# Digit counts for twelve columns at once, and two pairs of vector operations merged, in a fused attention, routing and MLP kernel

## The chip, the cores and the metric

One core of a Trainium2 chip runs the whole program. The metric is the device time of one execution in microseconds (us). The engines are named as in the profile: PE (TensorE; PEld is its weight loads), DVE (VectorE), ACT (ScalarE), POOL (GpSimd) and SP, whose queue issues the DMAs.

## The reference

Three stages follow each other, each on the output of the one before, all in float32:

```python
q_n, k_n = (rmsnorm(q, g_q), rmsnorm(k, g_k))        # 4 batches, 12 heads, 448 rows, 64 wide
attn = softmax(q_n @ k_n.T / 8)                      # per batch and head
x = (attn @ v)  laid out as 1792 rows of 768
order = np.argsort(-(x @ w_gate).flatten())          # 1792 tokens, 8 experts
for idx in order:                                    # a token takes its best expert that still
    tok, e = (int(idx) // E, int(idx) % E)           # has room; an expert holds cap = 224 tokens
    if assigned[tok] >= 0 or counts[e] >= cap:
        continue
    assigned[tok] = e
    counts[e] += 1
out[mask of e] = np.maximum(x[mask] @ w1[e], 0) @ w2[e]
h = out @ w_in;  result = (h * np.cos(h)) @ w_out    # 768 -> 2048 -> 768
```

The assignment must be exact: one swapped token changes whole rows of the result.

## The kernel before

**Attention** takes two heads (a pair) at a time, 24 pairs, 6 to a batch. Each pair has: squares and a root (`norm`, with a Newton iteration in `rsqrt`, lines 355 to 369) for the row norms of q and k; transposes (`turn`); a maximum per row (`shifts`: seven matmuls `s`, seven DVE reductions `cm`); scores, exponentials `pf` and their sums (`scores`, `weigh`); router logits of the pair, accumulated with the softmax sums in the one PSUM bank `dn`; reciprocals `r`, and the pair's output rows, transposed back into PSUM and scaled by `r` into `xk` (`tail`). A scaling of one pair is two DVE operations of 256 columns. Beside this work DVE, ACT and SP split the two MLP weights into high and low parts in pieces (`Narrow`, tiles `nr` and `na`, 38 pieces in this stage).

**Routing** needs for each expert its 224th best token. A token's logit is turned into an 18-bit and shorter digits; a histogram of the first digit comes from matmuls of two 0/1 matrices per column of 112 tokens (`ia == X` and `ib <= W`), 4 columns a batch. `Router.start` runs after the last pair of each batch: `best` (largest logit and its expert), `parts` (digits), `signs` (the two matrices of each column, half of the second ones as a sign on ACT; four matmuls into the bank `dn`) and an addition to `hist`. After batch 4, `quick` reads the histogram (`digits`: column totals `tot`, a matmul with `up`, a comparison `cmp`, a matmul with `ones`, a maximum `T`), and narrows to the next digit twice. The first routing stands between attention and the first expert with nothing beside it; the second one (expert 2) runs beside the first expert's matmuls, the others later.

**Order.** All steps are recorded, then a list planner (`Plan.run`) with its own costs writes each engine's instructions in the order it finds; the engines run their queues in that order. A change in any cost or count lets the planner place the whole attention stage anew. The second plan (experts and MLP) is laid out by itself.

Of the kernel before, what the change touches and what calls it, by code (L numbers as in the profile page):

```python
# [12 lines left out]
F32 = mybir.dt.float32  # L13
# [332 lines left out]
END = 20.0  # L346
NKQ = 5
NPA = 6
XKA = 0
XKL = 1  # L350
QND = False
SSA = 1


def rsqrt(v, out, x, t, g=None):
    v.tensor_scalar(out.bitcast(I32), x.bitcast(I32), 1, None, op0=ALU.logical_shift_right)
    v.tensor_scalar(out.bitcast(I32), out.bitcast(I32), -1, 0x5F3759DF, op0=ALU.mult, op1=ALU.add)
    for _ in range(3):
        if g is not None:
            g.tensor_tensor(t, out, out, op=ALU.mult)  # L360
            g.tensor_tensor(t, t, x, op=ALU.mult)
            g.tensor_scalar(t, t, -0.5, 1.5, op0=ALU.mult, op1=ALU.add)
            g.tensor_tensor(out, t, out, op=ALU.mult)
            continue
        v.tensor_tensor(t, out, out, op=ALU.mult)
        v.scalar_tensor_tensor(t, t, -0.5, x, op0=ALU.mult, op1=ALU.mult)
        v.scalar_tensor_tensor(out, t, 1.5, out, op0=ALU.add, op1=ALU.mult)


def attention(tc, P, R, ident, q, k, v, g_q, g_k, w_gate, x_dram, L, other):  # L370
# [4 lines left out]
    with ExitStack() as ctx:  # L375
# [30 lines left out]
        dns = ring("dn", 2, [128, CP])  # L406
        xks = ring("xk", 2, [CP, NC, 2 * UP * D])
        recs = ring("r", 3, [CP, NC, 2])
        abs_ = ring("ab", 1, [CP, 2, NC, 128], BF16)
        NPR = B * NP  # L410
        bt, b1, bs, bo, bd = bank("t", 2), bank("s1", 2), bank("st", 2), bank("po", 1), bank("dn", 1)

# [225 lines left out]
        def tail(P_, xk, e, r):  # L638
            xe, p = outs.pop(P_), bt()[0:CP]
            P.begin()  # L640
            for c in range(NC):
                pe.transpose(p[:, c * 128:(c + 1) * 128], xe[:, c * CP:(c + 1) * CP], ident)
            P.finish()
            for z in range(2):
                cs = slice(2 * z, 2 * z + 2)
                o = xk[:, cs, 2 * e * D:2 * (e + 1) * D].rearrange("p c (h d) -> p c h d", h=2)
                i = p.rearrange("p (c h d) -> p c h d", c=NC, h=2)[:, cs]
                if z < XKA or P_ >= NPR - XKL:
                    for c in range(2):
                        for h in range(2):  # L650
                            sc.activation(o[:, c, h], i[:, c, h], AF.Copy, scale=r[:, 2 * z + c, h:h + 1])
                else:
                    ve.tensor_tensor(o, i, r[:, cs].unsqueeze(3).to_broadcast([CP, 2, 2, D]), op=ALU.mult)

        roots_of, xk_of = {}, {}

# [20 lines left out]
        def finish(P_):  # L677
            if P_ < 0:
                return
            late = P_ >= NPR - LAST  # L680
            if P_ == NPR - 1:
                ve.tensor_reduce(part[:, :, :, H], part[:, :, :, 0:H - 2], AX.X, ALU.add)
            P.rush = END if P_ == NPR - 1 else 0.0
            r = rows(P_)
            if P_ % NP == NP - 1:
                b = P_ // NP
                ve.tensor_reduce(L[:, b * NC:(b + 1) * NC, :], part[:, :, :, (H - 2) * late:H + late], AX.X, ALU.add)
                R.start(abs_(), b)
            P.rush = 0.0
            pair(P_, r)  # L690

# [49 lines left out]

CP, NCOL, E, CAP = 112, 16, 8, 224
BIG = 1.5e38
SIGNS = 10
WIDE = 4096.0
SOON = 5.0
LATER = 10.0
# [3 lines left out]
class Router:  # L751
# [3 lines left out]
    def __init__(self, nc, pool, ident, L, rows):  # L755
# [32 lines left out]
        for s in range(8):  # L788
# [9 lines left out]
        iota(tmp[:, 144:272], [[-1, 128]], step=1)  # L798
        v.scalar_tensor_tensor(up.rearrange("p (e i) -> p e i", e=E), tmp[:, 144:272].rearrange("p (e i) -> p e i", e=E),
                               0.5, em.unsqueeze(2).to_broadcast([128, E, 16]), op0=ALU.is_ge, op1=ALU.mult)  # L800
        v.scalar_tensor_tensor(up, up.bitcast(F32), 2.0, self.ident, op0=ALU.mult, op1=ALU.add)


        row = t("row", [128, 1])
# [45 lines left out]
        v.tensor_copy(t("wd", [128, E]), w8)  # L850
        g.memset(t("rp", [128, 1]), float(CAP))
        g.memset(t("one", [128, 1]), 1.0)
        g.memset(t("rp2", [128, 1]), 2.0 * CAP)
        self.first_free()
        for name in ("m", "mx", "K", "F0", "F1", "Z", "X0", "X1", "X2", "W0", "W1", "W2", "G", "Q", "XF", "g"):
            t(name, [CP, NCOL])
        for name in ("X", "W"):
            t(name, [CP, NCOL, 2], BF16)
        for name in ("t0", "t1"):
            t(name, [CP, NCOL], I32)  # L860
# [1 line left out]
        t("hist", [128, 128])  # L862
        t("tot", [128, 2], F32R)
        t("acc", [128, 1])
        t("rpt", [128, 1])
        t("acc8", [128, E], BF16)
        t("cmp", [128, 128], BF16)
        for j in range(3):
# [66 lines left out]
    def parts(self, a, z, first=True, rest=True):  # L935

        P, v = self.P, self.nc.vector
        c = {n: P[n][:, a:z] for n in ("m", "mx", "K", "F0", "F1", "Z", "X0", "X1", "X2", "W0", "W1", "W2", "G", "t0", "t1")}
        k, K, i, j = c["m"].bitcast(I32), c["K"].bitcast(I32), c["t0"], c["t1"]
        if first:  # L940
            v.tensor_scalar(i, k, 31, -2147483648, op0=ALU.arith_shift_right, op1=ALU.bitwise_or)
            v.tensor_tensor(K, k, i, op=ALU.bitwise_xor)
        for q, (lo, n) in enumerate(((21, 7), (10, 7), (0, 6))):
            if not (rest if q else first):
                continue
            v.tensor_scalar(i, K, lo + n, 15, op0=ALU.logical_shift_right, op1=ALU.bitwise_and)
            v.scalar_tensor_tensor(c[f"X{q}"], c["mx"], -16.0, i, op0=ALU.mult, op1=ALU.add)
            v.tensor_scalar(j, K, lo, (1 << n) - 1, op0=ALU.logical_shift_right, op1=ALU.bitwise_and)
            v.tensor_scalar(c[f"W{q}"], j, 1.0 - (1 << n), None, op0=ALU.add)
        if not rest:  # L950
            return
        v.tensor_scalar(c["Z"], c["mx"], -16.0, 15.0, op0=ALU.mult, op1=ALU.add)
        for n, lo, z, add in (("F0", 21, 2047, 1.0), ("F1", 10, 0x3FFFFF, 2049.0), ("G", 0, 1023, 1.0)):
            v.tensor_scalar(i, K, lo, z, op0=ALU.logical_shift_right, op1=ALU.bitwise_and)
            v.tensor_scalar(c[n], i, add, WIDE, op0=ALU.add, op1=ALU.mult)
# [10 lines left out]
                                     row.rearrange("p (n k) -> p n k", k=2).unsqueeze(1).to_broadcast(sh),  # L966
                                     cols.unsqueeze(2).to_broadcast(sh), op=op)

    def signs(self, p, X, W, ab):

        nc, P = self.nc, self.P
        cols = X.shape[1]
        for c in range(cols):
            A, B, ib = ab[:, 0, c], ab[:, 1, c], P["ib"][0:CP]
            if c * SIGNS % 16 < SIGNS:
                nc.scalar.activation(B, ib, AF.Sign, bias=W[:, c:c + 1], scale=-1.0)
                nc.either("tensor_scalar", A, P["ia"][0:CP], X[:, c:c + 1], None, op0=ALU.is_equal)
            else:
                nc.either("tensor_scalar", B, ib, W[:, c:c + 1], 0.5, op0=ALU.is_le, op1=ALU.subtract)
                nc.either("tensor_scalar", A, P["ia"][0:CP], X[:, c:c + 1], 2.0, op0=ALU.is_equal, op1=ALU.mult)  # L980
            nc.tensor.matmul(p, A, B, start=(c == 0), stop=(c == cols - 1))

    def count(self, p, X, W, ab, n, whole=False):

        nc, P = self.nc, self.P
        for a in range(0, NCOL, 8):
            cs = slice(a, a + 8)
            self.match(ab[:, 0, cs], P["ia"][0:CP], X[:, cs], ALU.is_equal)
            self.match(ab[:, 1, cs, 0:n], P["ib"][0:CP, 128 - n:], W[:, cs], ALU.is_le)
            if whole:  # L990
                nc.begin()
            for c in range(a, a + 8):
                nc.tensor.matmul(p[:, 0:n], ab[:, 0, c], ab[:, 1, c, 0:n], start=(c == 0), stop=(c == NCOL - 1))
            if whole:
                nc.finish()

    def digits(self, p, n, T, signs=False):

        nc, P, v = self.nc, self.P, self.nc.vector
        rp = P["rp2" if signs else "rpt"]  # L1000
        if signs:
            v.tensor_copy(P["tot"], p[:, 0:1].to_broadcast([128, 2]))
        else:
            v.tensor_scalar(P["tot"], p[:, 0:1].to_broadcast([128, 2]), 0.5, None, op0=ALU.mult)
            v.tensor_tensor(rp, P["tot"][:, 0:1].bitcast(F32), P["rp"], op=ALU.add)
        pa = self.psum()
        nc.tensor.matmul(pa[:, 0:2], P["up"], P["tot"], start=True, stop=True)
        v.scalar_tensor_tensor(P["cmp"][:, 0:n], p[:, 0:n], pa[:, 0:1], rp.to_broadcast([128, n]), op0=ALU.add,
                               op1=ALU.is_ge, accum_out=P["acc"])
        v.tensor_scalar(P["acc8"], P["em"], P["acc"], WIDE, op0=ALU.mult, op1=ALU.mult)  # L1010
        pt = self.psum()
# [8 lines left out]
        v.tensor_tensor(P["X"], self.twice(P["XF"]), self.twice(P["Z"]), op=ALU.min)  # L1020
        v.scalar_tensor_tensor(P["W"], self.twice(F), T, self.twice(W), op0=ALU.is_equal, op1=ALU.mult)

    def start(self, ab, q):

        P, v, s = self.P, self.nc.vector, slice(4 * q, 4 * q + 4)
        self.best(self.L[:, s], s.start, s.stop, True)
        self.parts(s.start, s.stop, rest=q < 3)
        p = self.psum()
        self.signs(p[:, 0:128], P["X0"][:, s], P["W0"][:, s], ab)
        if q == 0:  # L1030
            v.tensor_copy(P["hist"], p[:, 0:128])
        else:
            v.tensor_tensor(P["hist"], P["hist"], p[:, 0:128], op=ALU.add)
# [1 line left out]
    def quick(self, first):  # L1035
# [4 lines left out]
        self.parts(12 * first, NCOL, not first)  # L1040
        if not first:
            p = ps()
            v.tensor_copy(P["X"], self.twice(P["X0"]))
            v.tensor_copy(P["W"], self.twice(P["W0"]))
            self.count(p, P["X"], P["W"], P["AB"], 128, True)
        self.digits(p, 128, T[0], first)
        self.narrow(P["F0"], T[0], P["X1"], P["W1"])
        p = ps()
        self.count(p, P["X"], P["W"], P["AB"], 128, not first)
# [514 lines left out]
```

## Time and profile before

| | us |
|---|---|
| median of 3 runs | 1137.42 (1134.14 to 1144.95) |
| profiled execution | 1139.09 |
| its span, first to last instruction | 1137.3 |
| attention, up to the last pair's logits | about 329 |
| first routing, up to the first gather of rows | about 329 to 357 |
| PE, DVE, ACT, POOL busy in the span | 1083.0, 873.6, 623.3, 248.6 |

Busy times are unions of spans. The matmuls' ends are modelled, so PE counts as busy while its pipeline only waits; the distance between equal matmuls of successive pairs is the better measure of pace. An idle time carries the engine whose result ended it.

### The profile page before, as it was taken

To read this page: it belongs to the slowest core of one execution; us is meant where nothing else is said; L and a number is where in the kernel's file an instruction comes from. 1 tells how busy PE (TensorE), PEld (TensorE's weight loads), DVE (VectorE), ACT (ScalarE), POOL (GpSimd) and SP (SyncE) were. 2 spreads that over 40 slices of the span, in tenths; PEclk is the share of its full clock that TensorE was granted. 3 is DMA by queue.
4 is the path that set the end of the run, shared out by engine and by line. 5 is a ranking of instruction groups with operands and counts; after the bars stand their busy time and mean duration, and the time that the engine had idled before them with its cause. 6 is when DMAs were issued, how large, how long until landed. Compare 5 with 4: busy or idle time off the path is not lost.

```text
span 1137.3 us, 20677 instructions
## 1 busy us (share of the span) xinstructions
PE 1083.0 (95%) x7272; PEld 880.7 (77%) x7272; DVE 873.6 (77%) x2250; ACT 623.3 (55%) x1512; POOL 248.6 (22%) x367
## 2 busy tenths in 40 slices
PE   7999999999966999999999999999999999999997
PEld 5555556555535898897988988899989798999887
DVE  7888989999988858999997885658889476856300
ACT  4787878865650337664566663337666236646300
POOL 3577777766511000000100000020000001000001
PEclk9899999999985899999999999999999999999999
DMA  6353455455653899789888669748866958666652
GB/s 146 106 156 113 147 185 163 163 163 180 210 215 94 237 217 304 254 230 371 282 222 199 226 211 283 243 155 219 230 207 221 323 195 235 193 217 210 240 185 93
DMA packets 172744, 234.34 MB, mean 206 GB/s; under 512 B 14112, under 2 KB 144608, under 8 KB 168032
## 3 DMA queue, kind: packets, MB, share of 16 engines
q1 hardware_dynamic: 170240, 222.01, 62.6%
q0 software_dynamic: 2400, 11.01, 3.0%
q8 instruction: 57, 0.93, 0.3%
q14 instruction: 47, 0.39, 0.1%
HBM read 196.37 MB, written 36.52 MB: 205 GB/s over the span
## 4 chain that ended last, share of the span: by engine, by line
PE 49%; DVE 10%; DMA 7%; issue 2%; SPq 1%; ACT 1%; POOL 0%; POOLq 0%; DVEq 0%; ACTq 0%
PE acc L47 47%; DMA ws<-in_moe_w_dram 3%; DVE wx L47 1%; PE rt L47 1%; DVE na L47 1%; DVE oh L47 1%; SPq L1301 1%; DMA ws<-in_moe_w_out_dram 1%; DMA xr<-x,idx 1%; PE tr L47 1%; DMA AB<-rows 1%; DMA wx<-w_out 1%; ACT wx L1310 1%; DVE AB L47 1%; DMA rows<-vm 1%
## 5 line engine op out<-in xcount | busy, mean ns | idle before, releaser
L47 PE MATMUL acc<-wx,gh 128*128 128x512 f32 (+1 forms) x896 | 226.8, 340 | 1.9 <-DMA wx<-w_out 1.9
L47 PE MATMUL acc<-x2h,wx 128*128 128x448 f32 x768 | 223.8, 369 | 0.0
L47 PEld LDWEIGHTS acc<-wx,gh 128*128 128x128 f32 x896 | 155.6, 190 | 22.6 <-issue 2.9
L47 PEld LDWEIGHTS acc<-x2h,wx 128*128 128x128 f32 x768 | 144.5, 188 | 11.5
L47 PE MATMUL acc<-wx,gl 128*128 128x512 f32 (+1 forms) x448 | 150.5, 336 | 0.0
L47 PE MATMUL acc<-x2l,wx 128*128 128x448 f32 x384 | 140.3, 365 | 0.0
L47 PE MATMUL acc<-gh,wx 128*128 128x448 f32 (+1 forms) x768 | 130.7, 326 | 4.0 <-DVE gh L47 2.9
L47 DVE TENSOR_TENSOR wx<-ws,wx 128x1024 fp32r<-128x1024 f32 (+1 forms) x96 | 104.6, 1089 | 33.8 <-ACT wx L1310 28.0
L47 POOL TENSOR_TENSOR pa<-pf,pf 112x448 f32<-112x448 f32 x94 | 111.7, 1208 | 71.9 <-ACT pf L47 71.7
L1261 POOL DMA_INDIRECT xr<-x,idx x16 | 17.4, 1085 | 502.6 <-DVE KX L47 133.9
L47 PEld LDWEIGHTS acc<-gh,wx 128*128 128x128 f32 x768 | 117.1, 192 | 12.9 <-DVE gh L47 3.2
L47 ACT ACTIVATE pf<-st 112x448 f32<-112x448 f32 x192 | 93.8, 539 | 42.0 <-PE st L47 40.4
L1310 ACT ACTIVATE wx<-ws 128x1024 fp32r<-128x1024 f32 (+1 forms) x96 | 91.0, 948 | 44.9 <-DMA ws<-in_moe_w_dram 23.1
L47 DVE TENSOR_REDUCE cm<-s 128x1 f32<-128x448 f32 x168 | 100.2, 619 | 18.7 <-PE s L47 16.6
L47 ACT ACTIVATE r<-r 128x448 f32<-128x448 f32 x128 | 74.0, 578 | 56.4 <-DVE r L47 54.5
L47 DVE SCALAR_TENSOR_TENSOR r<-r,acc 128x448 f32<-128x448 int32 (+1 forms) x128 | 77.7, 618 | 34.7 <-ACT r L47 33.5
L47 PE MATMUL acc<-xe,wx 128*128 128x448 f32 x576 | 91.9, 320 | 0.1
L47 PEld LDWEIGHTS acc<-wx,gl 128*128 128x128 f32 x448 | 85.0, 190 | 8.0
L47 PEld LDWEIGHTS acc<-xe,wx 128*128 128x128 f32 x576 | 86.2, 189 | 4.4 <-DVE wx L47 0.4
L47 PE MATMUL st<-qq,kk 64*112 64x448 f32 x576 | 88.7, 393 | 0.6 <-ACT pf L47 0.6
L47 ACT ACTIVATE oh<-oh 128x896 bf16<-128x896 bf16 x48 | 45.6, 950 | 75.9 <-DVE oh L47 75.8
L47 PE MATMUL po<-pf,vr 112*64 112x448 f32 x384 | 84.3, 555 | 0.0
(271 smaller groups left out, 1891.0 us busy)
## 6 DMA issues: line engine op xcount, KB each, us to landing
wx<-w_in SPq DMA_DIRECT2D x64, 768.0 KB
wx<-w_out SPq DMA_DIRECT2D x36, 1024.0 KB
ws<-in_moe_w_dram SPq DMA_DIRECT2D x64, 384.0 KB
ws<-in_moe_w_dram SPq DMA_DIRECT2D x48, 512.0 KB
nr<-in_moe_w_in_dram SPq DMA_DIRECT2D x32, 384.0 KB
w_in<-nr SPq DMA_DIRECT2D x32, 384.0 KB
ws<-in_moe_w_out_dram SPq DMA_DIRECT2D x14, 512.0 KB
w_out<-wx SPq DMA_DIRECT2D x14, 512.0 KB
```

The lines of the kernel that those rows point to most:

```text
L47: self.plan.add([(self.eng, self.plan.cost(self.eng, name, out, r, kw), lambda: f(*args, **kw), self.plan.shares(self.eng, name, out, r, k ...
L1261: P.add([("POOL", 2.1 - 0.9 * h, lambda x=x, h=h: nc.gpsimd.indirect_dma_start(out=x, out_offset=None, in_=x_rows, in_offset=bass.Indirect ...
L1301: nc.sync.dma_start(s, w[:, c0:c0 + 128].rearrange("(k p) n -> p k n", p=128))
L1310: P.add([("ACT", 0.093 + n * 0.1067, lambda: nc.scalar.activation(hi, s, AF.Copy)), ("DVE", 0.07 + n * 0.0667, lambda: nc.vector.tensor_co ...
```

## The change

1. `rsqrt`: the first guess is one operation on the integer, `-0.5 * bits + 0x5F3759DF`, not a shift and then a multiply-add.
2. `tail`: one DVE operation scales all four column blocks of a pair, where two scaled two each (the last pair stays on ACT).
3. `start`: nothing is counted after batches 1 and 2; after batch 3 the twelve columns of batches 1 to 3 are counted at once, after batch 4 its four. The matrices are made by DVE in 512-column operations (`match`), none on ACT, and the twelve matmuls stand in the queue as one block.
4. The first digits `X0` and `W0` are written twice side by side in bf16, so the later routings need no copy of them; counts are plain, so `up` and the thresholds `rp` need no factor of 2 and `digits` loses one small operation.

```diff
 def rsqrt(v, out, x, t, g=None):
-    v.tensor_scalar(out.bitcast(I32), x.bitcast(I32), 1, None, op0=ALU.logical_shift_right)
-    v.tensor_scalar(out.bitcast(I32), out.bitcast(I32), -1, 0x5F3759DF, op0=ALU.mult, op1=ALU.add)
+    v.tensor_scalar(out.bitcast(I32), x.bitcast(I32), -0.5, float(0x5F3759DF), op0=ALU.mult, op1=ALU.add)
...
-            for z in range(2):
-                cs = slice(2 * z, 2 * z + 2)
...
-                    ve.tensor_tensor(o, i, r[:, cs].unsqueeze(3).to_broadcast([CP, 2, 2, D]), op=ALU.mult)
...
+                ve.tensor_tensor(o, i, r.unsqueeze(3).to_broadcast([CP, NC, 2, D]), op=ALU.mult)
...
-                R.start(abs_(), b)
+                if b == 2:
+                    R.start(abs_(), 0, 12)
+                elif b == 3:
+                    R.start(abs_(), 12, 16)
...
-    def signs(self, p, X, W, ab):
-        for c in range(cols):
...
-                nc.scalar.activation(B, ib, AF.Sign, bias=W[:, c:c + 1], scale=-1.0)
-                nc.either("tensor_scalar", A, P["ia"][0:CP], X[:, c:c + 1], None, op0=ALU.is_equal)
...
-        for a in range(0, NCOL, 8):
-            cs = slice(a, a + 8)
+        step = 8 if cols == NCOL else 4
+        for a in range(0, cols, step):
+            cs = slice(a, a + step)
             self.match(ab[:, 0, cs], P["ia"][0:CP], X[:, cs], ALU.is_equal)
             self.match(ab[:, 1, cs, 0:n], P["ib"][0:CP, 128 - n:], W[:, cs], ALU.is_le)
+            if cols < NCOL and a + step < cols:
+                continue
...
-            v.tensor_scalar(P["tot"], p[:, 0:1].to_broadcast([128, 2]), 0.5, None, op0=ALU.mult)
-            v.tensor_tensor(rp, P["tot"][:, 0:1].bitcast(F32), P["rp"], op=ALU.add)
+        v.tensor_copy(P["tot"], p[:, 0:1].to_broadcast([128, 2]))
...
-        self.signs(p[:, 0:128], P["X0"][:, s], P["W0"][:, s], ab)
-        if q == 0:
+        self.count(p, P["X0"][:, s], P["W0"][:, s], ab, 128, a == 0)
+        if a == 0:
...
-            v.tensor_copy(P["X"], self.twice(P["X0"]))
-            v.tensor_copy(P["W"], self.twice(P["W0"]))
-            self.count(p, P["X"], P["W"], P["AB"], 128, True)
+            self.count(p, P["X0"], P["W0"], P["AB"], 128, True)
```

On DVE, behind the logits of batch 1 (`L`), the count stood before; now the same place has other work:

```order
L47 TENSOR_REDUCE L<-part 112x32
L47 TENSOR_TENSOR xk_223<-t_229,r_226 112x2x128
L47 TENSOR_REDUCE m<-L 112x4
L47 TENSOR_REDUCE cm_186<-s_230 128x1
L47 TENSOR_TENSOR oe<-L,m 112x32
L47 TENSOR_REDUCE cm_186<-s_231 128x1
L47 TENSOR_SCALAR m<-m 112x4
```

```order
L47 TENSOR_REDUCE L<-part 112x32
L47 TENSOR_REDUCE cm_184<-s_228 128x1
L47 TENSOR_SCALAR ss_171<-ss_171 112x48
L47 TENSOR_SCALAR rs_173<-ss_171 112x48
L47 TENSOR_REDUCE ss_172<-sq_169 112x8
L47 TENSOR_SCALAR na_239<-na_239 128x384
```

The same is true behind batch 2. Now DVE behind batch 3, with twelve columns (`X_123` and `W_124` are the first digits, `ab` the 0/1 matrices):

```order
L47 SCALAR_TENSOR_TENSOR X_123<-mx,t_127 112x24
L47 TENSOR_SCALAR W_124<-t_128 112x24
L47 SCALAR_TENSOR_TENSOR na_238<-nr_234,na_238 128x384
L47 TENSOR_TENSOR ab_225<-ia,X_123 112x512
L47 TENSOR_TENSOR ab_225<-ib,W_124 112x512
L47 TENSOR_TENSOR ab_225<-ia,X_123 112x512
L47 TENSOR_TENSOR ab_225<-ib,W_124 112x512
L47 TENSOR_TENSOR ab_225<-ia,X_123 112x512
L47 TENSOR_TENSOR ab_225<-ib,W_124 112x512
L47 TENSOR_REDUCE cm_184<-s_229 128x1
L47 TENSOR_REDUCE cm_185<-s_228 128x1
L47 COPY hist<-dn_233 128x128
```

Six operations of 512 columns stand where six of 128 (and two on ACT) stood. On PE the twelve matmuls of this count (three of them shown) stand behind one block of scores `st` more than the four did, and ahead of the pair's softmax sums in the same bank `dn`:

```order
L47 MATMUL st_231<-qq_154,kk_149 112x448
L47 MATMUL st_230<-sr_158,heads 112x448
L47 MATMUL st_231<-sr_158,heads 112x448
L47 LDWEIGHTS ab_225
L47 MATMUL dn_233<-ab_225 128x128
L47 LDWEIGHTS ab_225
L47 MATMUL dn_233<-ab_225 128x128
L47 LDWEIGHTS ab_225
L47 MATMUL dn_233<-ab_225 128x128
```

After attention PE, ACT, POOL and SP keep their order but for a handful of neighbours that change places.

## Rows read from the trace of the kernel before

**Rows 1.** The page: busy time of PE and DVE over the span.
```profile
PE 1083.0 (95%) x7272; PEld 880.7 (77%) x7272; DVE 873.6 (77%) x2250; ACT 623.3 (55%) x1512; POOL 248.6 (22%) x367
```
**Rows 2.** Windows in attention: PE, PEld, DVE, ACT, POOL busy, then PEclk, DMA.
```profile
166.00:178.00 12.00, 12.00 (x115) 7.07 (x111) 10.49 (x21) 10.14 (x36) 10.73 (x16) 1.00 0.37 123
238.00:250.00 12.00, 11.73 (x109) 6.59 (x110) 11.51 (x28) 7.75 (x18) 8.84 (x16) 1.00 0.39 134
262.00:274.00 12.00, 10.53 (x94) 6.68 (x92) 12.00 (x32) 7.09 (x16) 8.00 (x8) 0.86 0.53 158
```
**Rows 3.** PE's timeline: the logits of pairs 5, 10, 11, 17, 18, 19 (start, duration).
```profile
101.03 0.38 PE L47 MATMUL dn<-xe,wg 128*32 128x112 f32 x8
...
159.94 0.38 PE L47 MATMUL dn<-xe,wg 128*32 128x112 f32 x8
171.33 0.38 PE L47 MATMUL dn<-xe,wg 128*32 128x112 f32 x8
...
241.81 0.38 PE L47 MATMUL dn<-xe,wg 128*32 128x112 f32 x8
253.27 0.38 PE L47 MATMUL dn<-xe,wg 128*32 128x112 f32 x8
269.49 0.60 PE L47 MATMUL dn<-xe,wg 128*32 128x112 f32 x8
```
**Rows 4.** Timeline of the count after batch 3; in brackets idle before and its releaser.
```profile
257.67 1.56 POOL L47 TENSOR_TENSOR pa<-pf,pf 112x448 f32<-112x448 f32 x1
...
258.16 1.11 DVE L47 TENSOR_SCALAR m<-m 112x4 f32<-112x4 f32 x1
...
262.23 0.86 PE L47 MATMUL st<-qq,kk 64*112 64x448 f32 x6
...
265.36 1.04 PE L47 MATMUL dn<-ab 112*128 112x128 bf16 x4 [1.28 <-DVE ab L47]
...
266.33 1.36 PE L47 MATMUL st<-qq,kk 64*112 64x448 f32 x6
...
266.70 0.28 DVE L47 TENSOR_TENSOR hist<-hist,dn 128x128 f32<-128x128 f32 x1
```
**Rows 5.** DVE's groups by shape, 28 to 327 us: count, busy us, mean ns, idle before.
```profile
L47 DVE TENSOR_TENSOR xk<-t,r 112x256 f32<-112x256 f32 x46 | 17.4, 415 | 0.0
...
L47 DVE TENSOR_TENSOR qq<-t,qq 128x448 fp32r<-128x448 f32 x22 | 13.6, 618 | 0.8 <-ACT qq L47 0.6
...
L47 DVE TENSOR_SCALAR rs<-rs 112x48 int32<-112x48 int32 x7 | 1.6, 230 | 0.1
```
**Rows 6.** DVE's timeline: the first pair's Newton guess; the two scalings of a later pair.
```profile
7.00 0.86 DVE L47 TENSOR_SCALAR rs<-rs 112x8 int32<-112x8 int32 x2
7.53 0.54 DVE L47 TENSOR_TENSOR rt<-rs 112x8 f32<-112x8 f32 x2
...
209.27 0.74 DVE L47 TENSOR_TENSOR xk<-t,r 112x256 f32<-112x256 f32 x2
```
**Rows 7.** Timeline: the count after batch 4, and matches in the first routing.
```profile
331.12 0.18 DVE L47 TENSOR_REDUCE m<-L 112x4 f32<-112x32 f32 x1
...
333.07 0.94 PE L47 MATMUL dn<-ab 112*128 112x128 bf16 x4 [3.30 <-DVE ab L47]
...
333.41 0.25 DVE L47 TENSOR_SCALAR ab<-ia,X 112x128 bf16<-112x128 bf16 x1
...
334.04 0.29 DVE L47 TENSOR_TENSOR hist<-hist,dn 128x128 f32<-128x128 f32 x1 [0.38 <-PE dn L47]
...
342.84 0.42 DVE L47 TENSOR_TENSOR AB<-ib,W 112x512 bf16<-112x512 bf16 x1
...
343.18 1.28 DVE L47 TENSOR_TENSOR AB<-ia,X 112x1024 bf16<-112x1024 bf16 x2
```
**Rows 8.** Timeline of the second routing: a copy that goes, and PE's wait at the end.
```profile
356.30 0.17 DVE L47 CAST X<-X 112x32 bf16<-112x32 f32 x1
...
360.51 0.16 DVE L47 TENSOR_TENSOR rpt<-tot,rp 128x1 f32<-128x1 f32 x1
...
386.04 1.47 PE L47 MATMUL rt<-pv,oh 112*112 112x6 bf16 x16 [2.09 <-DVE pv L47]
```

## The prediction before the run

> **What bounds the kernel now.** I read the page first: PE is busy for 95% of the span and DVE for 77% [rows 1]. The shares mix stages, so I went on by stage. The change leaves the expert and MLP matmuls as they are; it touches attention (0 to 329 us) and the first two routings (329 to 388 us).
>
> In attention, look at windows of 12 us [rows 2]. PE has no gap in most of them, and DVE is at 10.5 us of 12 in one and 11.5 in another. Which of the two sets the pace? The logits' matmul of each pair is a mark that comes once a pair [rows 3]. From the fifth pair at 101.03 to the 18th at 253.27 there are 13 steps in 152.2 us, 11.71 us each. The step from 159.94 to 171.33 is 11.39 us, in the stretch where DVE has a gap of 13%; the one from 241.81 to 253.27 is 11.46 us, where DVE has a gap of 4%. A DVE with room does not make a pair shorter, so PE paces these pairs, and most of what DVE saves is idle time for it, or room for the weight splitting.
>
> One step is different: 253.27 to 269.49 is 16.2 us, 4.8 over 11.46. In it lies the count after batch 3 [rows 4]. PE stands for 1.28 us before the count's matmuls, and behind them the same six score matmuls take 1.36 us, not 0.86: the granted clock is 0.86 of full in that window [rows 2], against 1.00 in the two others, after PE had stood. The pair's softmax sums use the count's PSUM bank and so wait for `hist`. The time of this count is on the path; that of the counts after batches 1 and 2 is not seen in PE's waits.
>
> **The change part by part.** The sum is made against the profiled execution, 1139.1 us, 1.7 over the median of the three runs, 1137.4.
>
> *Newton's guess.* Eleven DVE operations go. In the first pair the two that go start at 7.00 and the multiplication behind them at 7.53 [rows 6]; this chain leads to the first transposes. It gains 0.53 us at most; nothing, if the multiplication's own start is held by something else. I take -0.4, near the row. The nine others (7 of 0.23 us [rows 5], two shorter) are about 1.9 us of DVE time beside PE.
>
> *Row scaling.* 46 operations become 23. Two take 0.74 us together [rows 6], one alone 0.415 [rows 5]. The nearest row to one of 512 columns that reads PSUM is `qq`, 448 columns in 0.618 us [rows 5]; 64 columns more at the same rate of about 1.04 ns make 0.685. That is 0.055 us a pair and 1.3 us for 23. The ends are no gain and 0.74 - 0.415 = 0.33 us a pair, 7.5 us; I take 1.3, since `qq` is the nearest in size and in what it reads. [...]
>
> *Counts after batches 1 to 3.* A count is 34 DVE operations: 6 in `best`, 21 in `parts`, 6 matrices, 1 addition. After batch 4 the 18 that come first stand back to back from 331.12 to 333.66 [rows 7], 0.14 us each; three counts are 102 of them, 14.3 us. In their place: 28 small ones, 3.9 us, and six matches of 512 columns at a pitch of 0.34 (342.84 to 343.18 [rows 7]), 2.0 us. DVE saves 8.4 us, and ACT six operations. With the two items above DVE is freed of 8.4 + 1.3 + 1.9 = 11.6 us.
>
> What of that shortens attention? Between nothing (PE paces) and 11.6 us (DVE paces). The slack that DVE could be guilty of is the distance of the mean step to the best, 11.71 - 11.39 = 0.32 us in 13 steps, 4.2 us. I take half of it, -2.1, since POOL and ACT have their part in such stalls.
>
> *The count after batch 3 itself* stays, for twelve columns. Between the digits and the last matrix stand six matches (2.0 us) where six short operations stood (0.14 each, 0.8): 1.2 us later. PE's queue has one block of scores more ahead of it, whose first six matmuls alone take 0.86 [rows 4]. I take +0.3, with ends -4.8 (the stall goes) and +4.8 (it doubles).
>
> *The count after batch 4* is on the path, with nothing beside it. Before, the six matrices took 6 x 0.14 = 0.8 us, from 332.8 to 333.66, matmuls already ran meanwhile, and the addition started at 334.04 [rows 7]. Now two matches take 0.34 + 0.42 = 0.76 us, to about 333.5, and only then four matmuls of 0.94 us together (the rate of this stretch) begin: the addition starts near 334.4. +0.3, ends 0 and +0.6.
>
> *Threshold operations* (`rpt`, five): each ran while PE multiplied with `up`, and `cmp` waits for PE. Zero in the first routing; if PE were faster the 0.16 us of each would be late. In the second routing DVE has the first expert's work too, and two copies and three `rpt` (0.16 and 0.17 us [rows 8]) are at most 5 x 0.14 = 0.7 us of its queue; half of it, 0.4, is what I take, since an `rpt` can lie beside PE. PE stands 2.09 us for the end of this routing [rows 8], so the 0.4 is on the path. One weight-splitting operation now stands between `tot` and `cmp`, another no longer ahead of `tot`: the total is the same. -0.4, ends -0.8 and +0.3.
>
> *Behind it* PE, ACT and SP keep their order, and all start earlier or later as a whole: 0.
>
> Sum: -0.4 - 2.1 + 0.3 + 0.3 - 0.4 = -2.3. 1139.1 - 2.3 = 1136.8 against the profiled execution, **1135 us** as a median.
>
> **The rivals.**
>
> *DVE paces attention after all.* For it: DVE is at 96 and 100% of two windows [rows 2], and the steps compared are only two. Against it: the equal steps [rows 3]. Then all 11.6 us come back: 1139.1 - 11.6 - 0.4 (start) - 0.1 (routings) = 1127, as a median 1125.
>
> *The twelve-column count stalls PE longer, and the change is slower.* Place: `dn<-ab` behind the third batch. In the count before, `m` of four columns took 1.11 us and ended when POOL's addition `pa` ended (257.67 + 1.56 against 258.16 + 1.11 [rows 4]), and not the 0.18 us of a small operation [rows 7]. Six matches could each meet such a POOL operation; three of them held for 1 us are 3 us, PE stands longer and then runs at the lower clock for longer. [...] Price: as much again as the stall before, +4.8, and the freed DVE time brings nothing: 1139.1 + 4.8 - 0.4 - 0.1 = 1143.4, as a median 1142. It decides from the point where the last match ends later than PE is through with the one block of scores more. Against it: POOL waits too, and the matrices of before went through the same contention 18 times.
>
> *The planner's new order of attention is worse by chance.* Every engine's queue there is laid out anew. Steps like that of 16.2 us could come in other pairs: two more would be +9.6, 1147 as a median. Or the one that is there could go: the range has it.
>
> **How the numbers follow.** The forecast (PE paces, a few us of slack) has 0.57, DVE as pace 0.20, the longer stall 0.15, the bad order 0.08. Its own range is 1130 to 1139: from all of the 4.2 us and half of the stall to none of the 4.2 and half a stall more. With the rivals, 1126 to 1143 leaves out half of the DVE case and the bad order. About 1%, 11.4 us, is what a measurement of this kernel can tell from no change; its own three runs lie 10.8 us apart. Faster by more: half of the DVE case and a little of the forecast's tail (the stall gone as well), 0.15. Slower by more: the tail of the last rival, 0.05. Within 1%: 0.80.
>
> **What would show it.** Right: the steps between the logits' matmuls of pairs 5 to 17 stay at 11.4 to 11.7 us while DVE has less to do there (or does its weight splitting earlier); the step of the count after batch 3 stays near 16 us, with `ab` as PE's releaser; 512-column scalings of about 0.69 us; the last pair's logits at about 326 us; the first routing from there to the first gather unchanged to 0.5 us. Steps near 11.0 would show DVE as the pace. A step above 19 us at the third batch, with matches near 1 us beside POOL's additions, would show the stall. What would make it wrong beside these: a queue order in attention that lets PE run dry at another place.

## The result, and the profile after

The changed kernel is slower, by 0.6%: 1144.86 us as the median of five runs (1138.08 to 1149.12), against 1137.42 for the kernel before on the same chip; the ratio is 1.0061, 95% interval 1.0035 to 1.0088. I had forecast 1135 and a range up to 1143. The profiled run of the change took 1144.86 us with a span of 1143.1, 5.8 us over the span before.

The page of the changed kernel first, the line that answers to [rows 1]:

```profile
PE 1082.6 (95%) x7272; PEld 879.4 (77%) x7272; DVE 864.2 (76%) x2136; ACT 620.8 (54%) x1504; POOL 250.8 (22%) x366
```

DVE is freed of 9.4 us (11.6 were forecast) and PE does the same work; still the span grew. The pair marks of [rows 3] in the change, pairs 1, 2, 5, 18 to 22 and 24:

```profile
51.84 0.40 PE L47 MATMUL dn<-xe,wg 128*32 128x112 f32 x8 [1.20 <-ACT xe L47]
66.28 0.38 PE L47 MATMUL dn<-xe,wg 128*32 128x112 f32 x8
...
103.36 0.38 PE L47 MATMUL dn<-xe,wg 128*32 128x112 f32 x8
...
255.77 0.38 PE L47 MATMUL dn<-xe,wg 128*32 128x112 f32 x8
274.13 0.38 PE L47 MATMUL dn<-xe,wg 128*32 128x112 f32 x8
281.70 0.38 PE L47 MATMUL dn<-xe,wg 128*32 128x112 f32 x8
295.52 0.38 PE L47 MATMUL dn<-xe,wg 128*32 128x112 f32 x8
310.00 0.38 PE L47 MATMUL dn<-xe,wg 128*32 128x112 f32 x8
...
332.07 0.40 PE L47 MATMUL dn<-xe,wg 128*32 128x112 f32 x8 [0.96 <-ACT xe L47]
```

Before, the marks that [rows 3] leave out are 52.52 and 63.05 (pairs 1, 2), 281.67, 295.89 and 306.75 (20 to 22) and 328.66 (24). So from pair 5 to pair 18 nothing changed: 152.4 us against 152.2. Pair 2 takes 14.44 us, not 10.53, and pair 22 takes 14.48, not 10.86. Pair 20 takes 7.57, not 12.18, and gives back more than pair 19 lost. From pair 1 to pair 24 the sum is 280.2 against 276.1 us, +4.1: +3.0 up to pair 5, +0.2 up to pair 18 and +0.9 behind it, so most of what pair 22 loses is given back by its neighbours.

Windows of the change: two at the start, two of [rows 2], and the one of pair 22 (columns as there).

```profile
10.00:20.00 10.00, 8.02 (x38) 4.02 (x37) 6.08 (x11) 2.62 (x5) 0.99 (x11) 0.76 0.67 164
...
52.00:60.00 8.00, 7.06 (x34) 3.73 (x27) 6.27 (x13) 5.32 (x12) 4.09 (x5) 0.57 0.25 100
238.00:250.00 12.00, 11.94 (x115) 7.01 (x111) 9.98 (x22) 7.90 (x19) 9.39 (x16) 1.00 0.56 186
262.00:274.00 12.00, 11.77 (x105) 6.87 (x105) 11.46 (x34) 6.15 (x15) 6.86 (x8) 1.00 0.29 90
296.00:308.00 12.00, 9.80 (x61) 5.08 (x60) 11.21 (x29) 5.14 (x12) 4.62 (x5) 1.00 0.68 217
```

The windows at pair 2 and pair 22 in the kernel before:

```profile
52.00:60.00 8.00, 8.00 (x63) 4.72 (x60) 7.01 (x15) 5.90 (x17) 6.36 (x8) 1.00 0.19 56
...
296.00:308.00 12.00, 12.00 (x118) 6.88 (x112) 11.15 (x29) 7.75 (x18) 5.84 (x6) 1.00 0.63 217
```

In 238 to 250 DVE now has a gap of 2 us, where it had 0.5, and the pairs there are no shorter. In 262 to 274, the count after batch 3, the clock is full, where it was 0.86. PE loses time in the other three windows. In 10 to 20 the granted clock is 0.76 and in 52 to 60, in pair 2, it is 0.57; before, the same windows had 1.00. But before had its own slow stretch, 0.84 in 36 to 44 and 0.73 in 44 to 52, where the change has 1.00, so up to the first logits nothing is lost. At pair 22 PE has a gap of 2.2 us, where before it had none (12.00 busy of 12). In windows of 0.5 us the clock of the change at pair 2 has two levels, 1.00 up to 52.5 us and from 59.5, and 0.50 from 53.0 to 59.0; the 0.57 is a mean over both. Six score matmuls `st` take 1.46 us at 54.84, and 0.87 at 60.26. PE's wait at pair 2 and its two longest at pair 22:

```profile
53.18 1.73 PE L47 MATMUL t<-ident,qn 112*128 112x112 f32 x8 [0.94 <-DVE kk L47]
...
299.42 0.47 PE L47 MATMUL s<-kk,qq 64*128 64x448 f32 x1 [1.24 <-DVE cm L47]
...
304.46 0.46 PE L47 MATMUL s<-kk,qq 64*128 64x448 f32 x1 [0.71 <-DVE cm L47]
```

The count after batch 3, in the change (answers to [rows 4]):

```profile
263.15 0.16 DVE L47 TENSOR_SCALAR m<-m 112x12 f32<-112x12 f32 x1
...
268.49 1.41 POOL L47 TENSOR_TENSOR qn<-qk,rs 112x512 f32<-112x512 f32 x1
268.92 1.26 DVE L47 TENSOR_TENSOR ab<-ia,X 112x512 bf16<-112x512 bf16 x1
270.10 0.41 DVE L47 TENSOR_TENSOR ab<-ib,W 112x512 bf16<-112x512 bf16 x1
...
271.15 1.14 PE L47 MATMUL dn<-ab 112*128 112x128 bf16 x12
```

One match of six is held by a POOL operation (it ends 0.28 us behind `qn`, and takes 1.26 us, not 0.41) and PE shows no wait for `ab`. DVE's scaling, the start of the first Newton chain, the count after batch 4 and the end of the second routing (answer to [rows 5] to [rows 8]):

```profile
L47 DVE TENSOR_TENSOR xk<-t,r 112x512 f32<-112x512 f32 x23 | 15.7, 682 | 0.0
```

```profile
6.87 0.24 DVE L47 TENSOR_TENSOR rt<-rs 112x8 f32<-112x8 f32 x2
...
337.51 0.58 PE L47 MATMUL dn<-ab 112*128 112x128 bf16 x4 [4.33 <-DVE ab L47]
338.13 0.29 DVE L47 TENSOR_TENSOR hist<-hist,dn 128x128 f32<-128x128 f32 x1 [0.67 <-PE dn L47]
...
389.84 1.00 PE L47 MATMUL rt<-pv,oh 112*112 112x6 bf16 x16 [1.60 <-DVE pv L47]
```

The account of the 5.8 us, by marks: -0.7 to the first logits, +4.1 to the 24th, +0.6 from there to the first gather (28.76 against 28.16), 0.0 to the second (33.49 against 33.54), +1.8 behind it.

### The profile page after: what moved, and what is told of

The parts are those of the page before. It is cut to its first block, busy times and chain, and to the rows that moved or that the text cites. A ratio compares the mean times of both kernels' runs of the same rounds, so it can differ in the third digit from the quotient of the medians.

```text
span 1143.1 us, 20551 instructions
## 1 busy us (share of the span) xinstructions
PE 1082.6 (95%) x7272; PEld 879.4 (77%) x7272; DVE 864.2 (76%) x2136; ACT 620.8 (54%) x1504; POOL 250.8 (22%) x366
## 4 chain that ended last, share of the span: by engine, by line
PE 48%; DMA 10%; DVE 8%; ACT 2%; issue 1%; SPq 1%; POOL 0%; POOLq 0%; ACTq 0%; DVEq 0%
PE acc L47 46%; DMA ws<-in_moe_w_dram 4%; DMA wx<-w_out 2%; DVE r L47 1%; DVE wx L47 1%; DMA AB<-rows 1%; PE rt L47 1%; DVE oh L47 1%; DMA ws<-in_moe_w_out_dram 1%; DMA xr<-x,idx 1%; ACT wx L1289 1%; PE tr L47 1%; SPq L1054 1%; DVE na L47 1%; DVE AB L47 0%
## 5 line engine op out<-in xcount | busy, mean ns | idle before, releaser
L47 PEld LDWEIGHTS acc<-gh,wx 128*128 128x128 f32 x768 | 116.2, 191 | 13.8 <-DVE gh L47 3.7
```

Source lines behind the costliest of these rows:

```text
L47: self.plan.add([(self.eng, self.plan.cost(self.eng, name, out, r, kw), lambda: f(*args, **kw), self.plan.shares(self.eng, name, out, r, k ...
```

## The experiments

Two theories to begin with. A: the list planner, given other steps, laid attention out anew, and the new order is worse; the new work costs nothing. B: the new work costs the time, the twelve-column count above all. Ratios are to the kernel before on the same chip, which was one for e1 to e4, another for e5 to e8 and e13 to e16, and a third for e9 to e12; a mark is the start of a pair's logits in the one profiled run.

**All of the change in the order of before (e1, again e9).** The planner gets the steps of before; at emission the second of two merged steps stands for both and the other emits nothing.

```
+    def swap(self, s, f):
+        s.ways = [(w[0], w[1], f, *w[3:]) for w in s.ways]
...
+    P.swap(P.steps[-2], lambda: None)
+    P.swap(P.steps[-1], lambda: v.real.tensor_scalar(out..., x..., -0.5, float(0x5F3759DF), ...))
...
-                if b == 2:
-                    R.start(abs_(), 0, 12)
-                elif b == 3:
-                    R.start(abs_(), 12, 16)
+                R.placed(abs_(), b)   # steps of before; batch 3's emit the 12 columns
```

> All of the change, but attention's instructions stand in the order in which the kernel before has them: the merged seed and the merged scaling take the place of the second of the two, the 12-column digits and matches the places of batch 3's, and the places of the counts after batches 1 and 2 stay empty. Theory A (the new order of attention costs the time, the new work does not): 0 to 4 us faster than before, 1133 to 1138 beside 1137, and some 8 us faster than the change; the logits of the second pair at 63 us as before, not 66; the step of the third batch's count near 16 us or less. Theory B (the work costs the time, the twelve-column count above all): as slow as the change, 1141 to 1147, with the loss at the third batch and the pairs behind it.

Measured: 1140.04 us, ratio 1.005 (1.0032 to 1.0068). The second pair's step is 10.55 us as before, all steps to pair 12 are within 0.25 us of before, but the step behind batch 3 is 17.95. Neither theory was met: slower than A allowed, and the pairs lose less than B wanted. Again, on another chip:

> The pinned kernel once more (all of the change, attention in the order of before), since its 1.005 and the 0.9996 and 1.0002 of its two halves do not fit together. Theory A (order alone): 0.997 to 1.002 this time, the first result a spread between series. Theory A2 (new durations upset the old order): 1.003 to 1.007 again, and then the two halves together do what neither does alone.

Measured: 1139.53, ratio 1.002 (0.9994 to 1.0047). The intervals overlap; what this kernel costs lies between nothing and 5 us. Its own two medians are 0.5 us apart. What differs is the kernel before, 1134.91 beside e1 and 1137.23 beside e9.

**Each part alone, order laid out anew (e2 seed, e3 scaling, e4 count).** Each is the kernel before with the lines of that part of the diff alone.

```
e2  -    v.tensor_scalar(..., 1, None, op0=ALU.logical_shift_right)
    -    v.tensor_scalar(..., -1, 0x5F3759DF, op0=ALU.mult, op1=ALU.add)
    +    v.tensor_scalar(..., -0.5, float(0x5F3759DF), op0=ALU.mult, op1=ALU.add)
e3  -            for z in range(2): ...
    +                ve.tensor_tensor(o, i, r.unsqueeze(3).to_broadcast([CP, NC, 2, D]), op=ALU.mult)
e4  +                if b == 2:
    +                    R.start(abs_(), 0, 12)
    ...
```

> The kernel before with the seed alone as one operation (11 DVE operations fewer); the order of attention is laid out anew. Theory A: the time goes by the order and can go either way by up to 5 us although work only goes away; if the second pair's logits come at 66 us as in the change, 2 to 4 us slower at that mark. Theory B: 0 to 2 us faster, the mark at 62.5 us.

> The kernel before with the row scaling alone as one operation a pair (23 DVE operations fewer); the order is laid out anew. Theory A: either way by up to 5 us, with the difference in one or two pairs' steps and not spread over all. Theory B: 0 to 2 us faster, spread evenly (0.06 us a pair).

> The change with the seed and the row scaling left as two operations each, so the twelve-column count and the lean routing alone; the order is laid out anew. Theory A: either way by up to 5 us; the second pair's logits at 63 us as before, since no count lies ahead of it. Theory B: most of the 7 us that the change lost, 1141 to 1146, lost at the third batch's count and behind it.

Measured: 1141.35 (1.0045; 1.0026 to 1.0064), 1144.68 (1.0088; 1.0068 to 1.0108) and 1142.58 (1.0068; 1.0048 to 1.0087). B falls for the first two: work only goes away, and the time rises by up to 10 us. e4 lies in B's range, but not where B put its loss: pairs 19 and 20, behind the count, take 25.4 us together (28.4 before), and its long step is pair 21's, 17.7 us against 14.2. Its second pair's logits come at 58.8 us, not at 63. The three losses add up to 23 us, the change lost 7: they are not prices of parts. In e3 the difference sits in single steps (13.8, 12.4 and 13.0 us at pairs 15, 17 and 22, where before had 12.1, 11.4 and 10.9); the mark that I named for e2, a late second pair, is not where its loss lies: that step is 11.3 us.

**No operation changed, another order (e5, e6).** One constant of the planner each.

```
e5  -SAME = 8.0
    +SAME = 9.0
e6  -        P.switch = 0.09
    +        P.switch = 0.095
```

> No operation changed: the kernel before with one of the planner's constants at 9.0, not 8.0 (the bonus for a PE step of the same matrix shape), so attention's instructions are the same and stand in another order. Theory A (the order costs): clearly off the time of before, and slower by 4 to 10 us as the single parts were, if the order of before is one of the good ones. Theory B (the new operations cost): within 2 us of before, either way.

> As the run with the other constant, by another one: the planner's cost of a change of matrix shape on PE at 0.095 us, not 0.090. All operations as before. Theory A: 4 to 10 us slower than before. Theory B: within 2 us.

Measured: 1142.38 (1.0049; 1.0028 to 1.0070) and 1142.56 (1.0048; 1.0025 to 1.0072). Every operation is that of before (2250 on DVE, as there), and the loss is most of the change's. So a new order alone is enough. Where these two lose it, one profile each does not settle: pairs 1 to 24 take 279.2 and 281.4 us (276.1 before), but the last logits come at 325.1 and 327.7 us, ahead of the 328.7 of before, since before loses time at its start, and the stretch behind them takes 812.6 and 812.8 us (808.6).

**The work by halves in the order of before (e7, e8).** The swaps of e1 for the seed and the scaling alone, and for the counts alone.

```
e7  R.placed(abs_(), b)  ->  R.start(abs_(), b)      # counts as before
e8  both P.swap of rsqrt and of the scaling left out
```

> The merged seed and the merged scaling in the order of before, the counts and the routing as before: 34 DVE operations and 3 us of DVE time go, and nothing else changes place. The pinned kernel with all parts was 5 us slower, which theory A did not expect. If the twelve-column count made that (theory B): this is 0 to 2 us faster than before. If instead any change of DVE's durations upsets an order laid out for the old ones (theory A2): slower by 2 to 6 us, although work only went away.

> The counts of the change (12 columns behind the third batch, and the lean routing) in the order of before, the seed and the scaling as two operations each. Theory B: carries the 5 us of the pinned kernel, 1138 to 1142. Theory A2: between before and the pinned kernel, 1134 to 1140, with no loss at the third batch's count itself.

Measured: 1137.53 (0.9996; 0.9979 to 1.0014) and 1136.85 (1.0002; 0.9978 to 1.0026). In the order of before neither half of the work costs or gains more than its interval. From pair 1 to pair 24 they take 275.9 and 276.9 us, before 276.1. The count does show in one step, 17.95 us behind batch 3 where e7 has 14.96 and before 16.22 (14.97 in e13, the kernel before with four setup operations moved), and about half of the 1.7 us comes back at pairs 13 and 15 (11.75 and 11.79 against 12.28 and 12.09), where the operations of the count after batch 2 are gone.

**The count a pair later (e10).** e1 with PE's count and the copy to `hist` 8 us of plan time later.

```
+            a[-1].shift = LATE * (q == 2)      # LATE = 8.0
...
-            out.append((st, idx[s], w[2]))
+            out.append((st + s.shift, idx[s], w[2]))
```

> The pinned kernel with one thing moved: PE's 12 matmuls of the count behind the third batch and the copy to hist stand a pair later in their queues (behind the logits of pair 19, ahead of the softmax sums of pair 20), when the matches have long been made. If PE's wait for the matches is what makes the step from pair 18 to pair 19 long (17.9 and 18.0 us in the pinned kernels, 16.2 before, 11.5 without a count): that step falls to 13 to 15 us and the kernel is 2 to 4 us faster than the pinned one, 1131 to 1135. If DVE's load there makes it: 17 to 18 us again and no gain.

Measured: 1140.80 (1.0032; 1.0011 to 1.0053). The step behind batch 3 falls to 12.88 us, and the next one rises to 19.07, where e9 has 12.48. PE's wait of e9, then DVE, POOL and PE of e10 at the matches:

```profile
264.58 0.38 PE L47 MATMUL dn<-ab 112*128 112x128 bf16 x4 [2.08 <-DVE ab L47]
```

```profile
263.30 0.41 DVE L48 TENSOR_TENSOR ab<-ia,X 112x512 bf16<-112x512 bf16 x1
263.63 1.35 DVE L48 TENSOR_TENSOR ab<-ib,W 112x512 bf16<-112x512 bf16 x1
264.90 1.34 DVE L48 TENSOR_TENSOR ab<-ia,X 112x512 bf16<-112x512 bf16 x1
266.17 1.26 DVE L48 TENSOR_TENSOR ab<-ib,W 112x512 bf16<-112x512 bf16 x1
267.35 0.68 DVE L666 TENSOR_TENSOR xk<-t,r 112x512 f32<-112x512 f32 x1
```

```profile
263.26 2.71 POOL L48 TENSOR_TENSOR pa<-pf,pf 112x448 f32<-112x448 f32 x2 [0.94 <-ACT pf L48]
265.93 1.22 POOL L48 TENSOR_TENSOR qn<-qk,rs 112x512 f32<-112x512 f32 x1
```

```profile
268.09 1.01 PE L48 MATMUL t<-ident,qn 112*128 112x112 f32 x4 [4.25 <-DVE xk L666]
```

```profile
264.00:276.00 12.00, 7.91 (x40) 5.02 (x40) 12.00 (x23) 3.63 (x8) 4.65 (x6) 0.72 0.53 169
```

Three matches of six are held for 0.9 us each beside POOL's two additions and its `qn`, DVE's scaling behind them is late, and PE stands 4.25 us for it instead of 2.08 for `ab` in e9. This is the mechanism of my second rival, three matches held, met in an order in which PE is ahead. In the window of that wait (the last row) DVE is busy for 12.00 us of 12. Taking away the wait for `ab` moved the loss by a pair and did not end it. That DVE has more to do there than the pair gives it room for is my reading and not shown: up to 2.7 us of its 12.00 are these holds.

**The change's work in two other orders (e11, e12).** The edits of e5 and e6 in the changed kernel.

> The changed kernel with the planner's constant at 9.0, not 8.0: its operations in another order. Theory A: anywhere from 1134 to 1150; 19 us between extremes is not expected, a difference of 2 us or more from the change is. Theory B: 1141 to 1147 as the change, since its operations are the same.

> The changed kernel with the planner's cost of a change of shape at 0.095 us, not 0.090: its operations in a third order. As for the one ahead: theory A, 1134 to 1150 and another time than its neighbours; theory B, 1141 to 1147.

Measured: 1140.05 (1.0020; 0.9992 to 1.0048) and 1148.29 (1.0114; 1.0076 to 1.0151). The same operations cost 8 us more or less by the order alone; the change (1.0061) lies between. The place is again not one: e11's pairs 1 to 24 take 275.4 us, less than before, but its first logits come at 54.6 us.

**The stall at the start (e13 to e16).** The first logits come at 45.7 us in one profile (e8) and at 50.7 in another of the same order (e7). DVE, POOL and PE of e7, and PE's windows:

```profile
35.00 1.24 DVE L47 SCALAR_TENSOR_TENSOR up<-tmp,em 128x128 fp32r<-128x128 f32 x1
...
36.38 1.11 DVE L47 SCALAR_TENSOR_TENSOR b<-it,ix 128x1 int32<-128x1 int32 x1
```

```profile
34.95 1.14 POOL L47 TENSOR_TENSOR pa<-pf,pf 112x448 f32<-112x448 f32 x1
...
36.34 1.13 POOL L47 TENSOR_TENSOR pa<-pf,pf 112x448 f32<-112x448 f32 x1
```

```profile
39.03 0.46 PE L47 MATMUL s<-kk,qq 64*128 64x448 f32 x1 [2.07 <-DVE cm L47]
```

```profile
36.00:42.00 6.00, 3.93 (x38) 2.37 (x40) 5.42 (x16) 2.98 (x17) 5.60 (x13) 0.79 0.06 9
42.00:48.00 6.00, 6.00 (x40) 2.86 (x34) 4.85 (x13) 3.20 (x12) 1.29 (x1) 0.64 0.58 147
```

And of e8, on the same chip:

```profile
34.88 0.28 DVE L47 SCALAR_TENSOR_TENSOR up<-tmp,em 128x128 fp32r<-128x128 f32 x1
...
35.21 0.24 DVE L47 SCALAR_TENSOR_TENSOR b<-it,ix 128x1 int32<-128x1 int32 x1
```

```profile
35.40 1.14 POOL L47 TENSOR_TENSOR pa<-pf,pf 112x448 f32<-112x448 f32 x1
```

```profile
36.00:42.00 6.00, 5.99 (x66) 3.39 (x66) 5.78 (x14) 5.33 (x28) 5.60 (x12) 1.00 0.01 3
42.00:48.00 6.00, 6.00 (x49) 3.32 (x47) 5.81 (x9) 3.94 (x9) 4.58 (x5) 1.00 0.62 153
```

`up` and `b` are setup operations of the router. In e8 both have started before POOL's addition does, and take 0.28 and 0.24 us. In e7 `up` comes 0.05 us behind the addition: it ends when that one has ended, `b` meets the next, PE stands 2.07 us for `cm`, and its granted clock over the window behind is 0.64. The first logits are 5 us apart, 50.67 against 45.68. The addition takes 1.14 us in both, so it lost nothing to `up` in e7. In e8 the hold went the other way round: POOL's small `rt` that started with `up` took 0.55 us, against 0.27 in e7. The stall is in the profile of before (`up` 1.24 us, PE's wait 2.16), though it has the same seed as e8, and in all four of that order with the merged seed (e1, e7, e9, e10). Edit, in before (e13), in e1 (e14) and in e7 (e15): `up`, `b`, the two that `b` reads and one more `ix` stand 1.5 us of plan time earlier; `up` reads its ramp from `hist`, which is not in use yet. e16 is e14 with 8 columns counted behind batch 2 and 4 behind batch 3.

```
+        nc.steps[-9].shift = nc.steps[-2].shift = nc.steps[-1].shift = SETUP     # ix, it, b; SETUP = -1.5
+        nc.steps[-10].shift = SETUP                                              # ix
...
+        nc.steps[-1].shift = SETUP                                               # up
e16 -        self.start(ab, *((0, 12) if q == 2 else (12, 16)))
    +        self.start(ab, *((0, 8), (8, 12), (12, 16))[q - 1])
```

> The kernel before with four of the router's setup operations (up, b and the two that b reads) 1.5 us of plan time earlier in DVE's queue, so that up and b no longer meet POOL's additions pa at 35 to 38 us; nothing else moves. If up and b held for 1.1 to 1.2 us each behind pa make PE's wait of 2.1 us for cm near 40 us and the half clock behind it (theory A3): that wait is gone, the first pair's logits come near 46 us and not at 49 to 52, and the kernel takes 1131 to 1134, 3 to 5 us less than before. If the stall only moves on: within 1 us of before.

> The pinned kernel (all of the change, the order of before) with the same four setup operations moved. The four profiles of pinned kernels with the merged seed all have the stall at 39 to 40 us, the one without it has none. Theory A3 (the merged seed starts POOL's chain 0.1 us earlier and so loses a race that before wins in part of its runs): first logits near 46 us, 1132 to 1136, 3 to 5 us less than the pinned kernel and 1 to 2 us over the kernel before with the same move, from the twelve-column count. If the stall is not from up and b: 1138 to 1140 as before.

> The merged seed and scaling in the order of before, the counts and the routing as before, the four setup operations moved. Theory A3: 1131 to 1134, 3 to 6 us less than without the move (1137.5), and within 1 us of the kernel before with the same move, since PE paces and DVE's 3 us are idle time.

> All of the change in the order of before with the setup operations moved, but batches 1 and 2 are counted together behind batch 2 (8 columns) and batch 3 by itself (4 columns). If the width of the count behind batch 3 made its step 1.8 us longer (17.9 and 18.0 us against 16.2 before): that step is 15 to 16.5 us and the kernel 1 to 2 us faster than with 12 columns there. If the merged operations as such did it: 17 to 18 us.

Measured: e13 1136.16 (0.9996; 0.9976 to 1.0016), e14 1135.19 (0.9992; 0.9972 to 1.0012), e15 1135.62 (0.9993; 0.9972 to 1.0014), e16 1138.61 (1.0024; 1.0004 to 1.0043). DVE and PE of e14:

```profile
33.24 0.29 DVE L822 SCALAR_TENSOR_TENSOR up<-hist,em 128x128 fp32r<-128x128 f32 x1
33.99 0.14 DVE L48 SCALAR_TENSOR_TENSOR b<-it,ix 128x1 int32<-128x1 int32 x1
34.88 1.17 DVE L48 CAST io<-tmp 112x112 bf16<-112x112 f32 x1
```

```profile
37.53 0.47 PE L48 MATMUL s<-kk,qq 64*128 64x448 f32 x1 [0.66 <-DVE cm L48]
```

The cast behind them is held now, but one hold is left of two, PE's wait is 0.66 us, the clock stays 1.00, and the first logits come at 46.2. e14 lies 4 to 5 us under the two series of e1, as expected; but those ran on other chips, and only the interval of the first is apart from e14's. It was also expected 1 to 2 us over e13, and lies 1.0 under it. e13 was expected 3 to 5 us faster than before and is not. Its PE's wait is down to 0.67 us, but its first logits come at 49.45: `up` starts at 36.46 us, in e14 at 33.24, so 3.2 us are lost ahead of the stall, by something that I did not follow. e15 gains nothing over e7 either (0.9993 against 0.9996; 1135.62 us, not 1131 to 1134). So the stall decides the first logits of single executions, and that it costs the kernel its median is not shown. In e16 the step behind batch 3 is 15.71 us, as the width would have it, but the one behind batch 2 is 14.13, not 11.71 as in e9, with PE's wait of 1.65 us for `cm`: the wide count costs wherever it stands, and the total did not gain.

No version beat the kernel before by more than its interval; e14, with all of the change in the old order but for the moved setup, is level with it.

## Why the prediction was wrong, point by point

**What bounds the kernel: right.** PE paces the pairs. DVE got room in 238 to 250 and the 13 steps stayed at 11.7 us on the mean. The first rival, that DVE paces, falls; but around the count of batch 3 PE does wait for DVE, 2.08 us for `ab` in e9 and 4.25 for `xk` in e10.

**Sizes.** The scaling of 512 columns takes 0.682 us, 0.685 was forecast. The two that it replaces took 0.74 [rows 6], so a pair saves 0.06 us. The first Newton chain is 0.66 us earlier at its first multiplication (6.87 against 7.53 [rows 6]), but the row of before is a late one. With two operations the seed has this multiplication at 7.05 to 7.09 us in e4, e5, e6 and e8, and at 7.53 to 7.86 in before, e3 and e13; merged, it stands at 6.84 to 7.02 in all eleven. The seed's own gain is thus 0.2 us where both are early. First logits spread over 45.7 to 54.8 us in the eighteen profiles, and 0.4 is lost in that. The -2.1 of the pairs' pace was 0. The count after batch 4: to `hist` 6.06 us behind the last logits, before 5.38 [rows 7], +0.7 where I took +0.3 with an end of 0.6; in the order of before (e14) the way to the first gather is 28.0 us and nothing is lost. The second routing gained 0.05 us, not 0.4, in a stretch that spans 32.8 to 35.2 us over the profiles. Behind it 0 was forecast and 1.8 came; over the profiles the stretch from the second gather's first transfer to the third's spans 134.4 to 139.8 us, so one profile does not show such a difference.

**The count after batch 3.** +0.3 was too small: in the old order (e1, e8, e9, e14) the step is 1.6 to 1.8 us longer than before and 2.8 to 3.0 longer than in e7; in the change it was +2.1 in that step and -4.6 in the next. Its ends held it. That POOL waits too is seen in before: `pa` takes 1.56 us beside `m` [rows 4], and 1.14 at 255.57.

**The step that failed** is one that I did not price. I wrote that every engine's queue in attention is laid out anew, gave that no term in the sum, and put it among the rivals at 0.08 with 9.6 us, as a bad chance. The order is where the change paid: +4.1 us between pair 1 and pair 24, with two steps of 14.4 us (3.9 and 3.6 longer than before), as that rival had it, and pair 19 longer by 2.1, of which pair 20 gave back 4.6; at pair 22 the new order let PE run dry, the sign that I had named last.

Two comparisons carry this. With the operations of before, a new order alone costs 5 us (e5, e6). With the operations of the change, the ratio goes from 1.002 to 1.011 in one series by the order alone (e11, e12, their intervals apart), and is 0.999 in e14, the old order with the setup moved. In the old order the new work stands at 0.9996 to 1.0002 by halves (e7, e8) and, in the two series of e1, at 1.005 and 1.002; so part of the change's 7 us can still be work that the old order does not carry well, up to 5 us by the first of the two. Eight orders laid out anew were run or given (the change, e2 to e6, e11, e12): their ratios are 1.002 to 1.011 and none is under 1, though e11's interval holds 1. That a new order costs about half a per cent was thus the likely case here, not one in twelve. Over the eighteen profiles the last logits come at 326.1 us on the mean of the ten in the order of before and at 329.2 on that of the eight in new ones, with 277.1 and 279.4 us for pairs 1 to 24; the groups overlap (275.9 to 279.2, and 275.4 to 282.5).

Still open: why the order of before is better than all eight (that it had been picked out as a fast one would do it, and is not shown); why e1's ratio differs between its series, which ran on different chips; and what sets the first microseconds of the start.

## What to carry to other kernels

Where a planner sets the order, an edit is two changes, the work and a new order; price the order by a run that changes nothing else, and the work by a run that keeps the old order. Time freed on an engine that does not pace returned nothing here (e7 and e15, with 34 DVE operations less, are level with before), and the new order that came with it cost more. Look at what small operations stand ahead of something that PE waits for: two of them, held behind another engine's operation, made PE stand for 2 us (e7), and moving them away shortened that wait to 0.7, though the kernel's median did not follow in e13 and e15.

## What the runs showed of the hardware that I had not expected

Whether a DVE operation of 0.28 us started 0.5 us ahead of a POOL addition or 0.05 us behind it made it last 0.28 or 1.24 us; with its neighbour, held in the same way, the first logits came 5 us later between these two executions, 2.07 of them PE standing, with a granted clock of 0.64 in the window behind. A cast with one source was held like `up` and `b` with two (1.24 and 1.11 us in e7): `io` takes 0.21 us in e8 and 1.17 in e14, where it starts 0.04 us behind POOL's `pa` and ends 0.07 behind it.
